# Backward attention scores with 64 streamed columns: a zero-padded dO that slides over eight output columns

## The chip, the core and the metric

The kernel runs on one NeuronCore of a Trainium2 chip. The time is the device time of one launch in microseconds (us). Six runs of the kernel before took 1149.5 to 1152.5 us, with a median of 1151.64 us. Lower is better.

The core has four engines that compute, each with its own in-order queue: TensorE (called PE in the profile, with its weight loads as PEld), VectorE (DVE), ScalarE (ACT) and GpSimd (POOL). SyncE (SP) issues the loads here, and POOL issues the stores. A matmul on PE is two instructions: a weight load of `lhsT`, and the matmul, which streams the columns of `rhs` past the weights and writes as many columns into PSUM.

## The reference

A small decoder with two layers that share their weights, batch 2, one query token, is run forward and then differentiated. Each layer is a grouped-query attention over a cache of 16384 keys, and an MLP. What is returned is the output and the gradients of nine inputs, the two caches among them.

```python
def _A_ref(x, k_cache, v_cache, wq, wo):          # Hq = 32, Hkv = 4, Sk = 16384, Dh = 128
    q = (x @ wq).reshape(B, Sq, Hq, Dh).transpose(0, 2, 1, 3)
    k = jnp.repeat(k_cache, rep, axis=1)           # rep = 8: eight query heads share a key head
    v = jnp.repeat(v_cache, rep, axis=1)
    scores = jnp.einsum("bhqd,bhkd->bhqk", q, k) * (Dh ** -0.5)
    p = _softmax(scores, axis=-1)
    o = jnp.einsum("bhqk,bhkd->bhqd", p, v)
    return o.transpose(0, 2, 1, 3).reshape(B, Sq, Hq * Dh) @ wo

x = x + _A_ref(_layernorm(x), ...)                 # layer 0
x = x + _B_ref(_layernorm(x), ...)                 # layernorm, gelu MLP
x = x + _A_ref(_layernorm(x), ...)                 # layer 1, same caches and weights
x = x + _B_ref(_layernorm(x), ...)
...
_out, _vjp = jax.vjp(_f, A_x, A_k_cache, A_v_cache, A_wq, A_wo, B_w1, B_b1, B_w2, B_b2)
```

The part that matters here is the backward pass through layer 1's attention. With dO the gradient of `o`, each key t of a head needs dP[h, t] = dO[h] . V[t], and from it dS = p * (dP - delta), and dq = sum over t of dS[h, t] K[t].

## The kernel before, in words

The work is cut by group: `g` is one pair of batch and key head, so there are G = 8 groups, and each holds eight query heads. A group's cache of 16384 keys by 128 is read in NCH = 4 chunks of 1 MB ([128 partitions, 32 blocks, 128]), a chunk is worked in NB = 4 slots, and a slot is eight blocks of 128 keys. The whole of layer 1's attention backward is `attn_bwd` (L597 to L713), and it has 8 x 4 x 4 = 128 slots. It runs from 504 us to 660 us of the profiled execution.

What a turn `s` of its loop emits, in the order in which PE's queue gets it:

1. `emit_T` (L420): eight transposes of the V chunk's blocks into one PSUM bank (L424, a matmul of 128 columns each, with the V block as weights and the identity streamed), and a copy of that bank to SBUF as `kT`, on ACT (L158) or DVE (L161), whichever a running charge of costs finds freer.
2. On every third turn one of the 16 transposes of a kept V chunk (`v_turns`, L326).
3. `sch.run_slot`: what was put off to this turn, most of all one `quad` of the dq sums (L456, eight matmuls of 256 columns with K as the streamed operand).
4. `score(s - 2)` (L670): the scores of the slot of two turns ago. Eight weight loads of `kT` blocks, and eight matmuls that stream dO of the group, eight columns, one for each head.
5. Once a chunk is complete, `post` (L638): one matmul that subtracts delta (L640), and one DVE multiplication that makes dS (`dX`, L646).
6. Work on the gradient of the normed input, as dot products on DVE (L343) and some transposes on PE (L326), taken from the queues `wq_q` and `dots`.

The last group, G - 1, has its V chunks held in SBUF (`keepV`, transposed in place), so its 16 slots need no transpose in this stage and are put between those of the third and fourth groups of the list.

The scores of a slot are written as follows; `sc[g, c]` is one PSUM bank seen as [128 keys of a block, 8 heads, 32 blocks], so that the eight results of a block are 32 floats apart:

```python
PE.matmul(sc[g, c][:, :, b * 8 + j], lhsT=kT[:, j, :], rhs=do_bf[:, g, :], start=(b + j == 0), stop=False)
```

K and V chunks, chunks of `wq` and later of the MLP's weights all take turns in NLD = 7 buffers of 1 MB (the pool `ld`). SP issues a load when its buffer's last reader is done: for a V chunk that is the last transpose of L424, for a K chunk the last matmul of L456, for a `wq` chunk the last dot of L343 with its sum (L617). The order of all this is written out by hand; nothing plans it at build time except the choice between ACT and DVE for copies.

Elsewhere the kernel streams more columns than it needs: in the products with weights (`wide_in` and `wide_out`, L175 to L181, used in L285, L367, L385 and L904) the two columns of the two batch rows are repeated 16 times, 32 columns in all.

Of the kernel before, what the change touches and what calls it, by code (L numbers as in the profile page):

```python
# [9 lines left out]
BF16 = mybir.dt.bfloat16  # L10
# [13 lines left out]
def kernel(  # L24
# [24 lines left out]
    nc = tc.nc  # L49
    V = nc.vector  # L50
    S = nc.scalar
    PE = nc.tensor
# [11 lines left out]
    G = B * HKV  # L64
# [14 lines left out]
    vec = ctx.enter_context(tc.tile_pool(name="vec", bufs=1))  # L79
# [12 lines left out]
    def pt(shape, dtype, name):  # L92
        return ps_tp.tile(shape, dtype, name=name, tag="tp")

    def px(shape, dtype, name):
        return ps_x.tile(shape, dtype, name=name, tag="x")
# [59 lines left out]
    def evac_bf16(dst, src, n):  # L156
        if pick() == "A":
            S.copy(out=dst.bitcast(I32), in_=src.bitcast(I32))  # L158
            charge("A", 0.17 + n / 2 / 1200.0)
        else:  # L160
            V.tensor_copy(out=dst, in_=src)  # L161
            charge("D", 0.16 + n / 1920.0)
# [159 lines left out]
    def turn(view, new_tp):  # L322

        tp = new_tp()
        for o in range(8):
            PE.transpose(tp[:, o, :], view[:, o * 128:(o + 1) * 128], ident[:])  # L326
        evac_bf16(view, tp[:].rearrange("p a b -> p (a b)"), 1024)
# [76 lines left out]
    def kept_vT(c):  # L404

        return held_tiles["V%d" % c][:].rearrange("p (t d) -> p t d", d=128)

    def kv_load(w, g, c):
        keep = w + str(c) if g == G - 1 else w if (g, c) == (XG, 0) else None
        t = held_tiles[keep] if keep else ld.tile([128, LDW], BF16, name="kv_" + w, tag="ld")  # L410
        if keep not in held:
            src = Kv if w == "K" else Vv
            nc.sync.dma_start(t[:].rearrange("p (t d) -> p t d", d=128), src[g, :, c * TC:(c + 1) * TC, :])
            if keep:
                held.add(keep)
        return t[:].rearrange("p (t d) -> p t d", d=128)
# [3 lines left out]
    def emit_T(cv, b, third):  # L420
        tp_n["n"] += 1
        tp = (px if third and tp_n["n"] % 3 == 0 else pt)([128, 8, 128], BF16, "tp")
        for j in range(8):
            PE.transpose(tp[:, j, :], cv[:, b * 8 + j, :], ident[:])  # L424
        kT = ktp.tile([128, 8, 128], BF16, name="kT", tag="kT")
        evac_bf16(kT[:].rearrange("p a b -> p (a b)"), tp[:].rearrange("p a b -> p (a b)"), 1024)
        return kT
# [169 lines left out]
    def attn_bwd(l, do_bf, dqT, dn, groups, ahead):  # L597
# [3 lines left out]
        for i, g in enumerate(groups):  # L601
            for c in range(NCH):
                for b in range(NB):
                    slots.append((g, c, b))
                    if 2 <= i < 2 + NCH // 2 and c % 2 == 0:
                        slots.append((G - 1, (i - 2) * 2 + c // 2, b))
        kTs, sc, accs = {}, {}, {}
        made = {"n": 0}
        done_g = []
        dots = deque()  # L610
# [27 lines left out]
        def post(g, c):  # L638
            dp = sc.pop((g, c))
            PE.matmul(dp[:].rearrange("p h t -> p (h t)"), lhsT=hot3[:],  # L640
                      rhs=dlr[:, g, l, :].unsqueeze(2).to_broadcast([128, 8, TC]), start=False, stop=True)
            k = made["n"]
            made["n"] += 1
            ds = dXr[k // 2 % 3][:, :, k % 2]
            ev = e_all[:, g, c * CP:(c + 1) * CP, l, :, :].rearrange("p a h b -> p h a b")
            V.tensor_tensor(out=ds.rearrange("p a h b -> p h a b"),  # L646
                            in0=dp[:].rearrange("p h (a b) -> p h a b", b=2), in1=ev, op=ALU.mult)
            charge("D", 0.5)
            if c == 0:
                def finish(ps, g=g):  # L650
                    V.tensor_scalar(out=dqT[:, g, :], in0=ps, scalar1=QSCALE, scalar2=None, op0=ALU.mult)
                    done_g.append(g % HKV)
                    if g == groups[-1]:
                        wq_n[g % HKV][1]()
                        wq_n[g % HKV][3]()
                    elif done_g.count(g % HKV) == 2:
                        by_dots(g % HKV)
                accs[g] = Acc(g, "K", None, finish, 2 if g == G - 1 else groups.index(g) % 2)
            acc = accs[g]
            if g == groups[-1]:  # L660
                accs[g].pre[c] = kv_load("K", g, c)
                if c == NCH - 1:
                    for k in range(NLD - 2):
                        ahead.load(k)
                        j0, rb = ahead.chunks[k]
                        w2_q.extend(lambda j=j: ahead.row(j) for j in range(j0, j0 + rb))
            coef = lambda u: ds[:, u - c * CP].rearrange("p h t -> p (h t)")
            sch.later(2, lambda: queue_acc(sch, acc, [c], c == NCH - 1, coef))

        def score(s):  # L670
            g, c, b = slots[s]
            if b == 0:
                sc[g, c] = px([128, 8, TC], F32, "dp")
            kT = kTs.pop(s)
            for j in range(8):
                PE.matmul(sc[g, c][:, :, b * 8 + j], lhsT=kT[:, j, :], rhs=do_bf[:, g, :], start=(b + j == 0),
                          stop=False)
            if b == NB - 1:
                post(g, c)

        cv = None
        s = 0
        v_turns = deque(lambda c=c, b=b: turn(held_tiles["V%d" % c][:, b * 1024:(b + 1) * 1024],
                                              lambda: pt([128, 8, 128], BF16, "turn"))
                        for c in range(NCH) for b in range(NB))
        while s < len(slots) + 2 or sch.busy():
            sch.s = s
            if s < len(slots):
                g, c, b = slots[s]
                if g == G - 1:  # L690
                    kTs[s] = kept_vT(c)[:, b * 8:(b + 1) * 8, :]
                else:
                    if b == 0:
                        cv = kv_load("V", g, c)
                    kTs[s] = emit_T(cv, b, True)
                    if s % 3 == 2 and s >= 8 and v_turns:
                        v_turns.popleft()()
                if g == groups[-1] and b == 1 and c == 0:
                    n = wq_n[g % HKV] = wq_steps(l, g % HKV, dqT, dn, lambda: pt([128, 8, 128], BF16, "wtq"),
                                                 lambda: px([128, 512], F32, "dn_ps"))  # L700
                    for k, f in enumerate(n[0]):
                        wq_q.append(lambda f=f, k=k, n=n: (f(), n[2][4 * k]()))
                        wq_q.extend(n[2][4 * k + 1:4 * k + 4])
            sch.run_slot(1 if s < len(slots) else 2)
            if 2 <= s < len(slots) + 2:
                score(s - 2)
            if wq_q and (s % 2 == 1 or len(wq_q) > 6):
                wq_q.popleft()()
            if dots and s % 3 < 2:
                dots.popleft()()  # L710
            s += 1
# [174 lines left out]
    def wq_steps(l, kv, dqT, dn, new_tp, new_ps, get_=None, done_=lambda *job: None):  # L886

        hs = slice(kv * 8, kv * 8 + 8)
        box = {}

        def load(j):
            wt = ld.tile([128, LDW], BF16, name="wqt", tag="ld") if get_ is None else get_("wq", kv, j)
            box[j] = wt[:].rearrange("p (j n) -> p j n", j=4)
            if get_ is None:
                nc.sync.dma_start(box[j], wq_v[:, j:j + 4, kv * D:(kv + 1) * D])

        def turn_row(j):
            turn(box[j - j % 4][:, j % 4, :], new_tp)

        def products(j0=0):  # L900
            ps = new_ps()
            for j in range(j0, DJ):
                for o in range(8):
                    PE.matmul(wide_out(ps, 2 * j), lhsT=box[j - j % 4][:, j % 4, o * 128:(o + 1) * 128],  # L904
                              rhs=wide_in(dq_all[:, kv * 8 + o, 2 * l:2 * l + 2]), start=(o == 0), stop=(o == 7))
            V.tensor_tensor(out=dn[:, j0:DJ], in0=dn[:, j0:DJ],
                            in1=ps[:, 2 * j0:2 * DJ].rearrange("p (j b) -> p j b", b=2), op=ALU.add)
            for j in (0, 4):
                done_("wq", kv, j)

        def dq_in():
            for b in range(2):
                V.tensor_copy(out=dq_all[:, hs, 2 * l + b], in_=dqT[:, b * HKV + kv, :])

        return [lambda j=j: load(j) for j in (0, 4)], dq_in, [lambda j=j: turn_row(j) for j in range(DJ)], products, box
# [353 lines left out]
    kTs, dps, accs, ready = {}, {}, {}, []  # L1269
# [126 lines left out]
    while 2 * m < NS + 12 or late or fill or late_pe or m <= max(v_at) + 2:  # L1396
# [6 lines left out]
        for k in range(2):  # L1403
            s = 2 * m + k
            if s < NS:
                i, b = NCH + s // NB, s % NB
                cv = get("V", *chunks[i])[:].rearrange("p (t d) -> p t d", d=128)
                kT = ktp.tile([128, 8, 128], BF16, name="kT", tag="kT")
# [55 lines left out]
```

## Time and profile before

| What | Value |
|---|---|
| Median of the runs (range) | 1151.64 us (1149.5 to 1152.5) |
| The profiled execution's own time | 1150.81 us |
| Its span (first to last instruction) | 1149.0 us |
| Mean granted PE clock over the span | 0.825 |
| Busy share of the span: PE, PEld, DVE, ACT, POOL | 83%, 64%, 55%, 49%, 6% |
| HBM read and written | 348.14 MB and 98.58 MB, 389 GB/s over the span |
| `attn_bwd`, matmuls of L676 | 896 from `kT` and 128 from `keepV`, 1024 in all, 504.4 to 657.2 us |

How to read it: the 1149.0 us are the span of one execution, which took 1150.81 us as a run, 1.81 us more than the span; the median of the six runs is 0.83 us above that run. A row of the windows view gives the length of a stretch and then the busy time of PE, PEld, DVE, ACT and POOL (with the number of instructions in brackets), the granted PE clock as a share of full speed, the busy share of the DMA engines, and GB/s. In the timeline a row is a start, a length, the engine, line and operation, and how many instructions are merged into it. The ends of matmuls are modelled, and each is longer than the spacing of two of them, so the spacing is read from starts: the start of one row against the start of the next.

### The profile page before, as it was taken

What the parts mean: (1) busy time and instruction counts of PE and PEld (TensorE: products, weight loads), DVE (VectorE), ACT (ScalarE), POOL (GpSimd) and SP (SyncE); (2) the same over time, 40 slices, a digit from 0 to 9 for tenths busy, and PEclk for the clock granted to TensorE, in tenths of its full rate; (3) what the DMA queues carried; (4) which work ended last, traced back from release to release, by engine and by line L of the source; (5) the groups of instructions that cost most, each with busy time, mean ns of one, the idle gap of its engine ahead of it and who ended that gap; (6) DMA issues with size and microseconds to landing.
All of it is one profiled execution on the core that took longest, in us unless ns stands there. A gap on an engine that the chain in (4) does not pass through costs nothing. (4 is left out here: it accounts for less than half of the span.)

```text
span 1149.0 us, 39958 instructions
## 1 busy us (share of the span) xinstructions
PE 958.0 (83%) x17581; PEld 733.0 (64%) x17581; DVE 632.4 (55%) x1335; ACT 566.9 (49%) x1417; POOL 63.7 (6%) x113
## 2 busy tenths in 40 slices
PE   4989795488879875899996889788898999999785
PEld 3867673487767765888775688665555555555452
DVE  1535451133535433454845355668777877786784
ACT  0544351022535430344554455657677867786673
POOL 0000000000000000000000000001111112111111
PEclk9988895597989875899998799888758967796785
DMA  9999999998999989999999999877999999999996
GB/s 374 423 424 425 425 424 412 408 362 366 423 424 416 423 310 424 387 357 406 366 421 420 357 357 359 322 292 295 383 416 416 421 422 420 424 423 419 423 422 253
DMA packets 89130, 449.30 MB, mean 391 GB/s; under 512 B 7026, under 2 KB 7026, under 8 KB 49788
## 3 DMA queue, kind: packets, MB, share of 16 engines
q1 hardware_dynamic: 72204, 348.17, 75.0%
q0 software_dynamic: 16752, 98.59, 20.7%
q8 instruction: 137, 2.24, 0.7%
q14 instruction: 37, 0.30, 0.1%
HBM read 348.14 MB, written 98.58 MB: 389 GB/s over the span
## 5 line engine op out<-in xcount | busy, mean ns | idle before, releaser
L158 ACT COPY kT<-tp 128x512 int32<-128x512 int32 x209 | 122.6, 586 | 253.6 <-PE tp L424 242.5
L161 DVE COPY kT<-tp 128x1024 bf16<-128x1024 bf16 x159 | 108.6, 690 | 113.0 <-PE tp L424 98.6
L424 PE MATMUL tp<-ident,kv_K 128*128 128x128 bf16 x1728 | 146.0, 234 | 4.2 <-DMA kv_K<-in_A_k_cache_dram 4.2
L424 PEld LDWEIGHTS <-kv_K 128*128 128x128 bf16 x1728 | 110.9, 105 | 5.0 <-DMA kv_K<-in_A_k_cache_dram 4.8
L169 DVE CAST big<-xm 128x512 bf16<-128x512 f32 x142 | 92.5, 685 | 28.9 <-PE xm L1242 13.3
L166 ACT CAST big<-xm 128x512 bf16<-128x512 f32 x155 | 84.5, 592 | 25.7 <-PE xm L1144 14.7
L577 PEld LDWEIGHTS <-kT 128*128 128x128 bf16 x2048 | 76.6, 98 | 28.6 <-issue 23.6
L577 PE MATMUL sc<-qT_bf,kT 128*128 128x8 bf16 x2048 | 92.1, 171 | 1.3 <-issue 1.3
L274 PE MATMUL wtp<-ident,wt 128*128 128x128 bf16 x928 | 76.4, 230 | 4.0 <-issue 2.5
L424 PE MATMUL tp<-ident,kv_V 128*128 128x128 bf16 x864 | 70.8, 230 | 8.6 <-DMA kv_V<-in_A_v_cache_dram 7.4
L541 ACT ACTIVATE e_all<-sc,negm 128x64 bf16<-128x64 f32 x256 | 76.9, 343 | 1.1 <-DVE negm L536 1.0
L310 PEld LDWEIGHTS <-wt 128*128 128x128 bf16 x1696 | 48.9, 103 | 44.2 <-issue 14.7
L169 DVE CAST keepK<-xm 128x512 bf16<-128x512 f32 x95 | 61.6, 684 | 16.5 <-PE xm L1242 10.7
L161 DVE COPY wT<-wtp 128x1024 bf16<-128x1024 bf16 (+1 forms) x64 | 40.5, 637 | 47.8 <-PE wtp L274 44.7
L456 PE MATMUL acc_all<-kv_V,e_all 128*16 128x256 bf16 x864 | 46.0, 293 | 24.8 <-DVE acc_all L439 12.3
L158 ACT COPY wT<-wtp 128x512 int32<-128x512 int32 (+1 forms) x60 | 34.5, 575 | 64.5 <-PE wtp L274 55.7
L166 ACT CAST keepK<-xm 128x512 bf16<-128x512 f32 x102 | 54.8, 592 | 21.8 <-PE xm L1242 21.1
L166 ACT CAST keepV<-xm 128x512 bf16<-128x512 f32 (+1 forms) x98 | 53.1, 592 | 22.1 <-PE xm L1242 19.9
L424 PEld LDWEIGHTS <-kv_V 128*128 128x128 bf16 x864 | 56.0, 102 | 10.5 <-DMA kv_V<-in_A_v_cache_dram 8.2
L274 PEld LDWEIGHTS <-wt 128*128 128x128 bf16 x928 | 58.6, 103 | 4.7 <-issue 3.4
L541 ACT ACTIVATION_READ_ACCUMULATOR e_all<-sc,negm 128x1 f32 x256 | 60.0, 235 | 0.0
L169 DVE CAST keepV<-xm 128x512 bf16<-128x512 f32 (+1 forms) x74 | 47.9, 684 | 16.7 <-PE xm L1242 12.8
(352 smaller groups left out, 1778.4 us busy)
## 6 DMA issues: line engine op xcount, KB each, us to landing
kv_K<-in_A_k_cache_dram SPq DMA_DIRECT2D x81, 1024.0 KB, 12.3
kv_V<-in_A_v_cache_dram SPq DMA_DIRECT2D x81, 1024.0 KB, 12.0
out_dram<-big POOLq DMA_DIRECT2D x36, 1024.0 KB, 16.1
wt<-in_A_wo_dram SPq DMA_DIRECT2D x32, 1024.0 KB, 9.3
wt<-in_B_w_dram SPq DMA_DIRECT2D x32, 896.0 KB, 14.2
out_dram<-keepK POOLq DMA_DIRECT2D x22, 1024.0 KB, 16.2
out_dram<-keepV POOLq DMA_DIRECT2D x18, 1024.0 KB, 15.8
wt<-in_A_wq_dram SPq DMA_DIRECT2D x16, 1024.0 KB, 8.6
```

Of the source, the lines that this page charges most:

```text
L158: S.copy(out=dst.bitcast(I32), in_=src.bitcast(I32))
L161: V.tensor_copy(out=dst, in_=src)
L166: S.copy(out=dst, in_=src)
L169: V.tensor_copy(out=dst, in_=src)
L274: PE.transpose(tp[:, o, :], wv[:, j, (o0 + o) * 128:(o0 + o + 1) * 128], ident[:])
L310: PE.matmul(fps[:, jo, :].rearrange("p (a b) -> p a b", b=2), lhsT=wv[:, j, jo * 128:(jo + 1) * 128], rhs=xT_bf[:, j0 + j, :].unsqueeze(1) ...
L424: PE.transpose(tp[:, j, :], cv[:, b * 8 + j, :], ident[:])
L456: PE.matmul(self.acc[cg:cg + 16, :], lhsT=coef(u), rhs=self.cv[:, t:t + 2, :].rearrange("p t d -> p (t d)"), start=False, stop=True, tile_ ...
L541: S.activation(out=e_all[:, g, f * half:(f + 1) * half, l, h, :], in_=sc[g][f][:, h, :].rearrange("p (a b) -> p a b", b=2), func=ACT.Exp, ...
L577: PE.matmul(sc[g][f][:, :, t % TH], lhsT=kT[:, j, :], rhs=q_bf[:, g, :], start=True, stop=True)
```

## The change

Three zeroed tiles `wide` of [128, 8 heads, 15] take the place of dO as the streamed operand. Two of them serve the seven groups that load V, in turn, and one serves the group G - 1. At the first slot of a group, DVE copies the group's dO into the middle column, number 7, of each head's 15. For block j the matmul streams columns 7 - j to 14 - j of each head: eight columns, of which the one at place j is dO and the others are zero. The output is then all eight columns of the slot for all eight heads, 64 columns, and each of the slot's eight matmuls adds onto the same 64 places of PSUM. Weight loads, the number of matmuls, the order of PE's queue and all loads and stores stay as they were.

```diff
-        kTs, sc, accs = {}, {}, {}
+        kTs, sc, accs, wide = {}, {}, {}, {}
+        for i, g in enumerate([G - 1] + groups):
+            wide[g] = vec.tile([128, 8, 15], BF16, name="wz%d" % i) if i < 3 else wide[groups[i - 3]]
+            if i < 3:
+                nc.gpsimd.memset(wide[g][:], 0.0)
...
             for j in range(8):
-                PE.matmul(sc[g, c][:, :, b * 8 + j], lhsT=kT[:, j, :], rhs=do_bf[:, g, :], start=(b + j == 0),
-                          stop=False)
+                PE.matmul(sc[g, c][:, :, b * 8:b * 8 + 8], lhsT=kT[:, j, :], rhs=wide[g][:, :, 7 - j:15 - j],
+                          start=(b + j == 0), stop=False)
...
+        wide_made = set()
...
                 if g == G - 1:
                     kTs[s] = kept_vT(c)[:, b * 8:(b + 1) * 8, :]
-                else:
+                if g not in wide_made:
+                    wide_made.add(g)
+                    V.tensor_copy(out=wide[g][:, :, 7], in_=do_bf[:, g, :])
+                if g != G - 1:
                     if b == 0:
                         cv = kv_load("V", g, c)
                     kTs[s] = emit_T(cv, b, True)
```

Lines after the first hunk move down by four, later ones by eight: the scores of L676 stand in L680 of the changed kernel.

## The prediction

> **What bounds the kernel now.** I first split the stage that holds the changed line by the windows view (columns: length, busy PE, PEld, DVE, ACT, POOL, PE clock, DMA share, GB/s), then asked for PE's waits in each part.
>
> ```profile
> 504.00:587.00 83.00, 79.64 (x1734) 65.71 (x1732) 47.34 (x106) 39.34 (x70) 0.00 (x0) 0.98 0.96 381
> 587.00:652.00 65.00, 49.45 (x915) 41.03 (x912) 35.50 (x78) 29.86 (x54) 0.00 (x0) 0.84 0.99 404
> 652.00:660.00 8.00, 7.43 (x137) 5.28 (x137) 0.42 (x1) 3.76 (x7) 0.00 (x0) 0.79 0.94 334
> ```
>
> PE's longest waits, with total, count and longest one; the first two of 504 to 587 us, the last two of 587 to 652:
>
> ```profile
> PE dp L676 <- DVE kT L161: 1.1, 1, 1.1
> PE acc_all L456 <- DVE acc_all L439: 0.7, 1, 0.7
> ...
> PE tp L424 <- DMA kv_V<-in_A_v_cache_dram: 7.4, 4, 3.7
> PE acc_all L456 <- DMA kv_K<-in_A_k_cache_dram: 2.9, 3, 1.3
> ```
>
> So the stage has three parts. To 587 PE never waits for a load: PE is the bound. From 587 to 652 it waits 12.3 us for loads (2.0 us on `wq` beside these two), with DMA at 0.99: the loads are the bound. From 652 on PE is busy 7.43 of 8 us again and ends the stage; its clock is 0.79.
>
> Where does PE's lateness in the first part reach the loads? Where DMA runs dry:
>
> ```profile
> 552.00:560.00 8.00, 7.92 (x177) 6.48 (x173) 6.89 (x15) 5.08 (x9) 0.00 (x0) 1.00 0.78 275
> 562.50:565.00 2.50, 2.50 (x65) 2.01 (x61) 2.43 (x6) 1.15 (x4) 0.00 (x0) 1.00 0.90 341
> 653.80:657.20 3.40, 3.40 (x57) 2.33 (x54) 0.00 (x0) 1.27 (x3) 0.00 (x0) 0.50 0.96 377
> ```
>
> The last dry stretch before the part bound by loads ends at 565 us. What PE is late by then moves all loads behind it; later lateness, up to the 640s, is taken up by PE's waits.
>
> **The price of 64 columns.** The timeline gives starts; the next row's start closes a set of eight.
>
> ```profile
> 551.26 0.36 PE L676 MATMUL dp<-doT_bf,kT 128*128 128x8 bf16 x8
> 551.47 0.34 PE L676 MATMUL dp<-doT_bf,keepV 128*128 128x8 bf16 x8
> 551.67 0.61 PE L424 MATMUL tp<-ident,kv_V 128*128 128x128 bf16 x8
> 552.12 0.61 PE L326 MATMUL turn<-ident,keepV 128*128 128x128 bf16 x8
> ...
> 487.10 0.36 PE L285 MATMUL do_ps_b<-gA_all,wT 128*128 128x32 bf16 x8
> 487.30 0.61 PE L274 MATMUL wtp<-ident,wt 128*128 128x128 bf16 x8
> ...
> 612.96 1.01 PE L424 MATMUL tp<-ident,kv_V 128*128 128x128 bf16 x8
> 613.77 0.41 PE L676 MATMUL dp<-doT_bf,kT 128*128 128x8 bf16 x8
> 614.03 0.37 PE L640 MATMUL dp<-dlr,hot 128*128 128x256 bf16 x1
> ```
>
> Eight score matmuls take 0.205 us (0.21 and 0.20), as do eight of 32 columns (0.20): below some width a matmul costs 25 ns whatever it streams. Eight of 128 columns take 0.45 us, 56 ns each. No row has 64. Half of 56 is 28, and 29 with a small fixed part: 0.23 us for eight, +0.03. The straight line between the rows of 32 and 128 gives 35 ns, +0.08. I take 29, for the 128-column row looks like pure streaming. At half clock (the last three rows) eight transposes take 0.81 us and eight scores 0.26; eight of 64 would take about 0.41, +0.15.
>
> A rule speaks against the change. The Trainium skill's "Advanced Engine Details and Errata", section "Memory Cachelines", says that the array's reads want at least two hits on a 16-byte line of SBUF, and that non-contiguous PSUM access slows matmuls, pairs being best. The new operand is read in runs of eight bf16 with 15 from run to run, mostly across a line's edge: two lines for each run instead of one. Were each line paid, 64 columns would cost twice, 56 ns, +0.25 us for eight. Against it stands the row: scores written one float at a time, 32 apart, already run at 25 ns, no slower than the contiguous L285, and the new writes are runs of eight. Nearly every line gets two hits or more. By the row the first part costs 1.9 us, by the rule 15; I keep the row, and the rule as a rival.
>
> **The change part by part.**
>
> 1. *Streaming, first part.* To 565 us the stage starts 496 score matmuls, 62 sets, all at clock 1.00: 62 x 0.03 = 1.9 us. PE has no cover there. Bounds: 0 (loads queued ahead absorb it) to 62 x 0.08 = 5.0 us. The 23 sets from 565 to 587 add 0.7 us of PE, covered by the load waits after 587.
>
> 2. *Streaming, second part.* About 39 sets, 1 to 4 us of PE, beside 12.3 us of waits for loads: nothing. If that cover went, it would be those 4 us.
>
> 3. *Streaming, tail.* From 640 us on DMA is dry at times (0.86 in 640.2 to 643.6) because buffers wait for PE. There lie four sets at half clock, 4 x 0.15 = 0.6 us.
>
> 4. *Eight DVE copies* of dO, 128x8 into a strided place. Nearest row: the cast L913, 128x8, 174 ns. Seven stand in DVE's queue two turns before PE needs them: nothing on PE, 1.2 us on DVE (47.34 of 83 us busy; it is full only around 555 to 575). The first one is different:
>
> ```profile
> 504.39 0.36 PE L676 MATMUL dp<-doT_bf,kT 128*128 128x8 bf16 x8
> 504.60 0.61 PE L424 MATMUL tp<-ident,kv_V 128*128 128x128 bf16 x8
> 505.42 0.27 DVE L942 MEMSET w2b_f<- 128x256 f32 x1
> 505.60 1.26 DVE L161 COPY kT<-tp 128x1024 bf16<-128x1024 bf16 x2
> 506.33 0.33 PE L676 MATMUL dp<-doT_bf,kT 128*128 128x8 bf16 x7 [1.12 <-DVE kT L161]
> ```
>
> DVE is in the delta chain (L870 to L882) until 505.1 and then clears two tiles. In the built order the first copy comes behind these and ahead of the `kT` copies. Until now the first scores waited for ACT's `kT` alone, at 504.39; now they wait for DVE, about 505.70 + 0.17, so 505.9. Queued behind them on PE are eight transposes (0.45 us) and the second scores, at 506.33 today because PE waits 1.12 us for DVE anyway: 505.9 + 0.23 + 0.45 = 506.6. So 1.5 us of new wait costs +0.3 us; late next are the transposes' buffers and with them loads, in a stretch where DMA is not full. Bounds 0.1 (the DVE copy alone) to 0.7.
>
> 5. *Three POOL memsets.* Emitted behind POOL's last work at 437.7 us, before the store at 700.53: idle engine, nothing; without that cover under a microsecond each (POOL's smallest rows take 0.5 to 0.7).
>
> No DMA, SP or ACT instruction is added or moved, and PE's queue keeps its order.
>
> **Sum.** 0.3 + 1.9 + 0.6 = 2.8 us. The profiled execution took 1150.81 us (span 1149.0 and 1.81 around it): 1153.6. The median is 0.83 us above it: **1154.4 us**, +0.24%. Everything after 660 us starts from this stage's gradient, so I pass the delay on whole.
>
> **The clock.** The low steps of the granted clock last multiples of 3.4 us and follow stretches where PE streams little. The skill's "TensorE: Matmul & The Clock Gate", Part 1, states such a window and that activity lifts the clock; columns streamed in zeros are activity too. By the row nothing changes; by the rule some of these steps go. Counted from the trace for the window before 653.8: 16 transposes, a 256-column matmul and a quad (four at a time) stream about 2800 columns of the 7800 that fit at 56 ns for 128, 36%; one wide set there adds 448, to 42%. The same count over the whole trace has windows that keep full clock from 35% up and windows that lose it up to 44%: undecided. What one saved step is worth: in the tail two sets of transposes (0.71 and 0.94 us against 0.45 each) and two quads (0.54 against 0.32 each), 1.2 us.
>
> **Rivals.**
>
> - *The tail stays warm.* Part 3 falls to 0.1 and 1.2 us come back: 0.3 + 1.9 + 0.1 - 1.2 = +1.1, **1152.7**, within 0.2%. For it: the 42%. Against: one set can miss the window.
> - *Faster: the clock.* The steps at 571.9, 640.2 and 653.8 all go, 3 x 1.2 = 3.6 us, and loads queued ahead absorb part 1's streaming (a K or V load lands 12 us after its issue, so there is a queue): 0.3 - 3.6 = -3.3, **1148.3**. It decides where the lateness that reaches the loads stays below about 1 us. Against: DMA did run dry at 552 to 560, and faster PE in the middle gains nothing.
> - *Dear columns.* 35 ns gives 5.0 + 0.3 + 1 = 6.3, **1158**; the line rule at 56 ns gives 15 + 0.3 + 2, **1169**. For it: the rule, and no row of 64. Against: flat cost to 32 columns.
>
> That the change does not do what it says is excluded: the built list shows 1024 matmuls of 8x8 columns in the old places.
>
> **How the numbers follow.** Under 0.2% (2.3 us, 1149.3 to 1153.9) a measurement of this kernel tells nothing apart. Forecast 0.40 (own range 1153.2 to 1156.5, 0.30 of it above 1153.9); tail warm 0.27; faster 0.18; dear columns 0.15. So slower 0.30 + 0.15 = 0.45, same 0.10 + 0.27 = 0.37, faster 0.18. For eight in ten the range takes half of the faster case and the cheaper half of the dear one: 1148.5 to 1160.
>
> **What would show it.** Starts of eight wide scores 0.23 us apart at full clock (0.28 or more speaks for dear columns); the first scores near 505.9; DMA drier around 552 to 560 by nearly 2 us, PE's waits for loads after 587 shorter by 1 to 4 us; the stage's end near 662.5. Fewer half-clock steps between 568 and 658 speak for the clock rivals. The forecast is wrong if the loads' queue hides the first part, or if the clock settles the tail.

## The result and the profile after

The changed kernel is slower. Its median is 1157.86 us (15 runs, 1153.55 to 1160.73) against 1151.79 us of the kernel before in the same series. The ratio over all runs is 1.0045, with a 95% interval of 1.0033 to 1.0058: +5.2 us on the time before, from 3.8 to 6.7 (the two medians alone lie 6.1 us apart). The forecast was 1154.4, +2.8. The sign and the range (1148.5 to 1160) held, but the loss is nearly twice the forecast's, and above the forecast's own range of 1153.2 to 1156.5.

The profiled execution took 1157.91 us, its span is 1156.1 us (before: 1149.0) and its mean granted clock 0.826 (0.825). I measured the changed stage from the start of the second of its two delta matmuls (L864, now L872; 502.94 us before, 503.94 after) to the first of the 64 products with `wq` that follow the last scores (L904, now L912; 661.14 and 666.82). It took 158.2 us before and 162.9 us after, +4.7. The other 2.4 us of these two executions lie outside: 1.0 before the stage, where only the three memsets are new (0.47 us in all, on an idle POOL), and 1.4 behind it, where nothing is.

The windows view of the profile after, with the columns of before, cut at the same three parts of the stage:

```profile
505.00:588.00 83.00, 80.73 (x1671) 67.93 (x1669) 46.86 (x107) 37.32 (x66) 0.00 (x0) 1.00 0.93 361
588.00:656.40 68.40, 53.17 (x979) 45.33 (x977) 36.74 (x85) 31.84 (x58) 0.00 (x0) 0.89 1.00 405
656.40:664.00 7.60, 7.60 (x113) 5.82 (x113) 0.42 (x1) 2.68 (x5) 0.00 (x0) 0.64 0.84 278
```

In the same 83 us PE gets through 1671 matmuls instead of 1734, is busy longer (80.73 for 79.64), and DMA moves 361 GB/s instead of 381. The parts keep their bounds: PE first, then the loads (DMA 1.00), then PE alone at a low clock.

PE's waits after, the first three in 505 to 588 us (the whole list there), the last two the longest waits on K and V in 588 to 656.4:

```profile
PE dp L680 <- DVE wz L699: 1.3, 1, 1.3
PE acc_all L456 <- DVE acc_all L439: 0.7, 1, 0.7
PE o_ps L471 <- DVE dX L650: 0.2, 1, 0.2
...
PE tp L424 <- DMA kv_V<-in_A_v_cache_dram: 8.1, 4, 3.7
PE acc_all L456 <- DMA kv_K<-in_A_k_cache_dram: 2.1, 3, 0.9
```

The first line is the new wait for the dO copy. It stands where the wait of 1.1 us for DVE's `kT` stood. No other wait came in in this part. Two waits of the list before (504 to 587 us) shrank; the second of them lies ahead of 565 us:

```profile
PE o_ps L471 <- DVE dX L646: 0.6, 1, 0.6
PE tp L424 <- DVE kT L161: 0.6, 1, 0.6
```

The timeline of PE after: two wide sets at full clock, with the row that closes them, and one at half clock.

```profile
553.07 0.45 PE L680 MATMUL dp<-wz,kT 128*128 128x64 bf16 x8
553.35 0.43 PE L680 MATMUL dp<-wz,keepV 128*128 128x64 bf16 x8
553.62 0.61 PE L339 MATMUL dotr<-ident,dq_all 128*128 128x128 bf16 x8
...
658.72 0.61 PE L680 MATMUL dp<-wz,kT 128*128 128x64 bf16 x8
659.14 1.04 PE L424 MATMUL tp<-ident,kv_V 128*128 128x128 bf16 x8
```

Eight scores take 0.28 and 0.27 us, 34 ns a matmul, where the forecast had 29. At half clock they take 0.42, as forecast (0.41). In the median of the stage's sets at full clock it is 0.277 us against 0.213, +0.064: 62 sets are 4.0 us instead of 1.9.

How late PE is can be read directly. The 63rd set of scores is the first behind 565 us; its row before, and after:

```profile
565.15 0.36 PE L676 MATMUL dp<-doT_bf,kT 128*128 128x8 bf16 x8
```

```profile
569.91 0.44 PE L680 MATMUL dp<-wz,kT 128*128 128x64 bf16 x8
```

Counted from the delta matmul it starts at 62.21 us before and at 65.97 after: PE is 3.76 us late at the end of the part in which the forecast gave it no cover. This is the main reading. The working comes out: 62 x 0.064 = 4.0, and 0.2 of the first wait, less 0.4 that the old wait for DVE's `kT` gave back (0.57 us before, 0.13 after).

The start of the stage in the timeline after:

```profile
506.60 0.17 DVE L699 COPY wz<-doT_bf 128x8 bf16<-128x8 bf16 x1
506.62 0.68 DVE L161 COPY kT<-tp 128x1024 bf16<-128x1024 bf16 x1
506.83 0.44 PE L680 MATMUL dp<-wz,kT 128*128 128x64 bf16 x8 [1.27 <-DVE wz L699]
...
507.55 0.44 PE L680 MATMUL dp<-wz,kT 128*128 128x64 bf16 x8
```

The first scores start 2.89 us after the delta matmul, before it was 1.46: 1.43 us late, as the forecast had it (1.5). The second scores start 3.61 us after it, before it was 3.40: 0.2 us are left of the wait.

Where DMA ran dry, in the windows view before:

```profile
552.00:565.00 13.00, 12.92 (x297) 10.10 (x293) 11.78 (x24) 7.33 (x14) 0.00 (x0) 1.00 0.85 316
```

And after, the same 13 us of the stage (it starts 1.0 us later), and the low clock in the tail:

```profile
553.00:566.00 13.00, 12.99 (x280) 10.57 (x273) 10.13 (x22) 6.22 (x11) 0.00 (x0) 1.00 0.74 273
655.10:661.90 6.80, 5.53 (x64) 4.32 (x64) 0.35 (x3) 2.16 (x4) 0.00 (x0) 0.50 0.70 237
```

DMA's share in these 13 us fell from 0.85 to 0.74, which is 1.4 us of all queues. SP issues the loads later, for it waits for PE's reads: of the 25 us from 546 on it waited 11.3 us for L456 and 9.3 for L424. The last loads of this stretch, before and after:

```profile
563.98 1.61 SPq L413 DMA_DIRECT2D kv_K<-in_A_k_cache_dram  x2
```

```profile
568.30 2.05 SPq L413 DMA_DIRECT2D kv_K<-in_A_k_cache_dram  x2
```

From the delta matmul that is 61.04 and 64.36 us: the loads are 3.3 us late as well. The low step of the clock at 571.9 is gone, but the one in the tail is 6.8 us long instead of 3.4.

### The profile page after: what moved, and what is told of

It is laid out like the page before. It is cut to its first block, busy times and chain, and to the rows that moved or that the text cites. A ratio compares the mean times of both kernels' runs of the same rounds, so it can differ in the third digit from the quotient of the medians.

```text
span 1156.1 us, 39970 instructions
## 1 busy us (share of the span) xinstructions
PE 966.2 (84%) x17581; PEld 744.3 (64%) x17581; DVE 633.7 (55%) x1343; ACT 567.1 (49%) x1417; POOL 64.2 (6%) x116
## 3 DMA queue, kind: packets, MB, share of 16 engines
q0 software_dynamic: 16752, 98.59, 20.5%
## 5 line engine op out<-in xcount | busy, mean ns | idle before, releaser
L424 PE MATMUL tp<-ident,kv_K 128*128 128x128 bf16 x1728 | 146.5, 235 | 3.3 <-DMA kv_K<-in_A_k_cache_dram 3.2
L424 PEld LDWEIGHTS <-kv_K 128*128 128x128 bf16 x1728 | 111.3, 105 | 4.0 <-DMA kv_K<-in_A_k_cache_dram 3.8
L424 PE MATMUL tp<-ident,kv_V 128*128 128x128 bf16 x864 | 68.9, 225 | 9.2 <-DMA kv_V<-in_A_v_cache_dram 8.1
L456 PE MATMUL acc_all<-kv_V,e_all 128*16 128x256 bf16 x864 | 46.2, 294 | 28.4 <-DMA kv_V<-in_A_v_cache_dram 16.9
L166 ACT CAST keepV<-xm 128x512 bf16<-128x512 f32 (+1 forms) x98 | 53.1, 593 | 20.5 <-PE xm L1250 18.6
L424 PEld LDWEIGHTS <-kv_V 128*128 128x128 bf16 x864 | 55.3, 101 | 10.8 <-DMA kv_V<-in_A_v_cache_dram 9.5
```

The source lines that it names most:

```text
L166: S.copy(out=dst, in_=src)
L456: PE.matmul(self.acc[cg:cg + 16, :], lhsT=coef(u), rhs=self.cv[:, t:t + 2, :].rearrange("p t d -> p (t d)"), start=False, stop=True, tile_ ...
```

## The experiments

The expectations set theories against each other: that the price of the streamed columns is the loss; that it is the wait and the copies; that it is where the new tiles push everything behind them in SBUF. All ratios are to the kernel before on the same chip. "A set" is eight score matmuls of a slot at full clock, "the stage" as measured above, and "late" is how much later the 63rd set starts after the delta matmul than in the kernel before. The diffs are cut to what matters; `...` marks what is left out.

### Eight columns again, the rest of the change kept

```diff
-                PE.matmul(sc[g, c][:, :, b * 8:b * 8 + 8], lhsT=kT[:, j, :], rhs=wide[g][:, :, 7 - j:15 - j],
+                PE.matmul(sc[g, c][:, :, b * 8 + j], lhsT=kT[:, j, :], rhs=wide[g][:, :, 7],
```

> The changed kernel with eight streamed columns again, read from the middle column of the padded tile; the eight DVE copies, the three memsets and the new wait of the first scores stay. Theory S (streaming of 64 columns on PE, 34 ns a matmul against 25.6, is the loss): eight scores take 0.205 us, the time is that of the kernel before plus 0.3 us, about 1152. Rival W (the copies and waits on DVE are the loss): it stays near the changed kernel, about 1157.

Measured: 1154.0 us, ratio 1.0031 (1.0017 to 1.0046). A set takes 0.22 us and the wait of 1.3 us for `wz` is there. The result lies between the theories. In its profile PE is only 0.4 us late (the single elements 15 apart are a little slower than the 0.21 of before, and 0.15 us of the wait is left); the interval of the loss begins at 2.0 us. The stage took 160.2 us, +1.9, and the work outside it 3.3 us more than in the profile before, so that most of this execution's loss lies where nothing was changed. Where it comes from stays open. The run shows that narrow columns take away nearly all of PE's lateness; how much of the time they take back it does not show.

### Half as many columns

```diff
-            wide[g] = vec.tile([128, 8, 15], BF16, name="wz%d" % i) if i < 3 else wide[groups[i - 3]]
+            wide[g] = vec.tile([128, 8, 7], BF16, name="wz%d" % i) if i < 3 else wide[groups[i - 3]]
...
-                PE.matmul(sc[g, c][:, :, b * 8:b * 8 + 8], lhsT=kT[:, j, :], rhs=wide[g][:, :, 7 - j:15 - j],
+                t0, k = b * 8 + j - j % 4, 3 - j % 4
+                PE.matmul(sc[g, c][:, :, t0:t0 + 4], lhsT=kT[:, j, :], rhs=wide[g][:, :, k:k + 4],
...
```

> The padded tile is seven wide, and a matmul streams 32 columns (four output columns of each head). Theory S: below the floor of 25 ns width is free, eight scores take 0.205 us, about 1152. Rival R (the padded layout costs, not the width: runs that cross lines): 28 ns or more a matmul, 1154 to 1156. Rival C (the granted clock, lifted by padded columns, moves the time): fewer half-clock steps than before, and a time below 1151.

Measured: 1163.26 us, ratio 1.0101 (1.0078 to 1.0123). No theory of the stage expected this. A set takes 0.21 us, so 32 columns cost no more than eight. But the stage starts at 508.9 us instead of 502.9: six microseconds were lost before the first changed score ran. What differs there is the size of the padded tiles, and with it the address of everything allocated behind them. That led to the two runs with an unused tile further down.

### Which layout costs: operand contiguous, PSUM in single floats

```diff
-            wide[g] = vec.tile([128, 8, 15], BF16, name="wz%d" % i) if i < 3 else wide[groups[i - 3]]
+            wide[g] = vec.tile([128, 15, 8], BF16, name="wz%d" % i) if i < 3 else wide[groups[i - 3]]
...
-                PE.matmul(sc[g, c][:, :, b * 8:b * 8 + 8], lhsT=kT[:, j, :], rhs=wide[g][:, :, 7 - j:15 - j],
-                          start=(b + j == 0), stop=False)
+                PE.matmul(sc[g, c][:, :, b * 8:b * 8 + 8].rearrange("p h t -> p t h"), lhsT=kT[:, j, :],
+                          rhs=wide[g][:, 7 - j:15 - j, :], start=(b + j == 0), stop=False)
...
```

> 64 columns, but the padded tile is laid out with the heads innermost, so each matmul reads 64 neighbouring elements; its PSUM writes are then single floats 32 apart. Theory S with the width alone as cause: 34 ns a matmul as in the changed kernel, about 1158. Rival R (the operand's runs across lines cost): 29 ns, eight scores in 0.23 us, about 1154.5. Rival P (PSUM places apart cost): more than 34 ns, over 1160.

Measured: 1169.39 us, ratio 1.0154 (1.0129 to 1.0180), stage 175.3 us. PE's timeline:

```profile
560.62 0.62 PE L680 MATMUL dp<-wz,kT 128*128 128x64 bf16 x8
561.05 0.64 PE L680 MATMUL dp<-wz,keepV 128*128 128x64 bf16 x8
```

The starts are 0.43 us apart, 54 ns a matmul (53.8 in the mean over the stage at full clock): the same 64 columns, each written to a float 32 floats from the last, cost nearly twice 29. It is also a dose run. With +0.22 a set the kernel lost 17.7 us instead of 5.2. PE is 13.8 us late, which is 62 x 0.22 and 0.2 of wait; the rest comes later, for PE's first wait of over 0.4 us for a load comes only 122 us into the stage (before: 90). The time follows the price of the set.

### Both contiguous

```diff
-            wide[g] = vec.tile([128, 8, 15], BF16, name="wz%d" % i) if i < 3 else wide[groups[i - 3]]
+            wide[g] = vec.tile([128, 15, 8], BF16, name="wz%d" % i) if i < 3 else wide[groups[i - 3]]
...
-                sc[g, c] = px([128, 8, TC], F32, "dp")
+                sc[g, c] = px([128, TC, 8], F32, "dp")
...
-                PE.matmul(sc[g, c][:, :, b * 8:b * 8 + 8], lhsT=kT[:, j, :], rhs=wide[g][:, :, 7 - j:15 - j],
-                          start=(b + j == 0), stop=False)
+                PE.matmul(sc[g, c][:, b * 8:b * 8 + 8, :], lhsT=kT[:, j, :],
+                          rhs=wide[g][:, 7 - j:15 - j, :], start=(b + j == 0), stop=False)
...
```

The delta matmul (L644) and the multiplication (L650) read the bank in its new order; the multiplication takes 422 ns as before.

> 64 columns, operand and PSUM writes both contiguous (the scores' bank is laid out block by block with the heads innermost; the DVE product reads it with a stride). Width alone: 34 ns, about 1158. Rivals R or P: 29 ns, about 1154.5; together with the run that has only the operand contiguous this tells which of the two.

Measured: 1154.6 us, ratio 1.0020 (1.0007 to 1.0034), stage 159.3 us. A set takes 0.24 us, with matmuls 29.0 ns apart in the median: the forecast's price is right for contiguous columns. The same copies, the same wait, the same 64 columns, and PE is 1.6 us late instead of 3.8; the ratio fell by about half.

### Is it the address? An unused tile

```diff
+    spare = vec.tile([128, 384], BF16, name="spare")
+    nc.gpsimd.memset(spare[:], 0.0)
     x1 = attn_layer_fwd(0, xT0)
```

In the kernel before, 768 bytes a partition of it put the load buffers 256 bytes past a multiple of 512, where the change put them; 384 bytes put them 384 past one. In the changed kernel and in the contiguous one, 256 bytes put them back on a multiple of 512; the runs of the next three sections carry these 256 bytes too.

> The kernel before with one unused tile of 768 bytes a partition, which moves the load buffers, caches and work tiles up by as much as the three padded tiles do in the changed kernel (start of the buffers 256 past a multiple of 512). Theory S (streaming is the whole loss): no change, 1151.5. Rival A (where the load buffers start matters): slower, by up to the 2.7 us that the run with eight columns was over the kernel before.

> The kernel before with one unused tile of 384 bytes a partition, which moves the load buffers as the 32-column version does (384 past a multiple of 512). Theory S: no change, 1151.5. Rival A: about 1161 to 1163, for the 32-column version took 1163 although its matmuls were at 25 ns, and its 8 KB packets took 312 to 321 ns against 309 before.

> The changed kernel with 256 bytes more, so that the load buffers start at a multiple of 512 again, as before. Theory S: no change, 1157.9. Rival A: down by what the address costs, to 1155 to 1156; what is left over the kernel before is streaming and the new wait.

> 64 columns with operand and PSUM contiguous, and the load buffers at a multiple of 512. By my sum with 29 ns a matmul: 2.8 us over the kernel before with the tail at half clock, 1154; 1.1 us over with the tail warm, 1152.7. Rival A says it is below the same version without the extra 256 bytes (1154.6).

Measured: 768 bytes in the kernel before, 1151.7 us, 1.0002 (0.9988 to 1.0016). The changed kernel put back, 1155.71 us, 1.0044 (1.0028 to 1.0059), the same ratio as without. So no part of this change's loss is seen to come from the address. Put back, its profile loses in the stage nearly what the first one did (162.2 us, before 158.2; PE is again 3.8 us late), while the work outside the stage takes 991.2 us against 990.8.

384 bytes, in a kernel with no other change: 1166.3 us, 1.0130 (1.0103 to 1.0157). The windows view of one stretch ahead of the stage, before and with 384 bytes:

```profile
100.00:400.00 300.00, 240.87 (x5087) 204.88 (x5086) 120.15 (x282) 106.03 (x446) 2.07 (x3) 0.81 1.00 409
```

```profile
100.00:400.00 300.00, 238.06 (x5010) 201.77 (x5007) 117.88 (x275) 103.88 (x442) 2.07 (x3) 0.81 0.99 402
```

The DMA is as busy and moves 1.7% less, where the loads are the bound. The run with half as many columns has its buffers at the same place and moved 403 GB/s there; the address accounts for what it lost ahead of the stage.

The contiguous kernel put back: 1154.86 us, 1.0029 (1.0016 to 1.0043), +3.3 us. PE's timeline:

```profile
551.14 0.41 PE L680 MATMUL dp<-wz,kT 128*128 128x64 bf16 x8
551.38 0.40 PE L680 MATMUL dp<-wz,keepV 128*128 128x64 bf16 x8
```

The starts are 0.24 us apart. The prediction's sum, 2.8 us, was made with about this price (0.23), and the kernel with this price lost 2.3 and 3.3 us in its two forms. The number agrees; its parts are less sure. PE is 1.6 us late in both profiles, and the stages (159.3 and 159.8 us) are hardly longer than in kernels that lose nothing (158.9 to 159.6, below).

### PSUM contiguous, operand in single elements

```diff
-                PE.matmul(sc[g, c][:, :, b * 8:b * 8 + 8], lhsT=kT[:, j, :], rhs=wide[g][:, :, 7 - j:15 - j],
+                PE.matmul(sc[g, c][:, b * 8:b * 8 + 8, :], lhsT=kT[:, j, :],
+                          rhs=wide[g][:, :, 7 - j:15 - j].rearrange("p h t -> p t h"),
...
```

The bank is laid out as in the contiguous kernel.

> 64 columns with contiguous PSUM writes, but the operand read one element at a time, 15 apart (columns outer, heads inner, over the changed kernel's padded tile); load buffers at a multiple of 512. Theory P (places apart in PSUM make a matmul dear, the operand's layout does not): 29 ns, eight scores in 0.23 us, time as with both contiguous, 1154.9. Rival R (the operand's layout does): over 34 ns, for every element lies on another line, and 1158 or more.

Measured: 1226.27 us, ratio 1.0661 (1.0632 to 1.0690). PE's timeline:

```profile
563.70 1.09 PE L680 MATMUL dp<-wz,kT 128*128 128x64 bf16 x8
564.61 0.65 PE L680 MATMUL dp<-wz,keepV 128*128 128x64 bf16 x4
```

0.91 us a set, 114 ns a matmul. PE is 46 us late and bounds nearly the whole stage: of its waits for loads (14.9 us before) 1.4 us are left, behind 200 us of the stage. The idea that only the PSUM side can cost fell: elements of the operand 15 apart cost four times what contiguous ones do. Where the granted clock was 0.50 a matmul took 117 ns, nearly the same.

### The copies alone

The change's tiles, memsets and copies are in; the scores still stream eight columns of dO and wait for no copy.

```diff
+                if g not in wide_made:
+                    wide_made.add(g)
+                    V.tensor_copy(out=wide[g][:, :, 7], in_=do_bf[:, g, :])
```

> Memsets and the eight copies of the changed kernel, but the scores stream dO itself, eight columns, and wait for no copy; load buffers at a multiple of 512. Theory S: as the kernel before within 0.5 us, 1151.7. Rival W (the copies' own time on DVE is a part of the loss): as the run with eight columns from the padded tile, 1153 to 1154.5.

Measured: 1152.4 us, ratio 1.0010 (0.9993 to 1.0026), stage 158.9 us. Copies and memsets cost nothing that can be measured; the interval's ends are -0.8 and +3.0 us. PE is not late at all (0.0 us). The interval overlaps that of the run with eight columns from the padded tile.

### Wide scores in the last three groups only

```diff
+                if g in groups[4:]:
+                    PE.matmul(sc[g, c][:, :, b * 8:b * 8 + 8], lhsT=kT[:, j, :], rhs=wide[g][:, :, 7 - j:15 - j],
+                              start=(b + j == 0), stop=False)
+                else:
+                    PE.matmul(sc[g, c][:, :, b * 8 + j], lhsT=kT[:, j, :], rhs=do_bf[:, g, :], start=(b + j == 0),
+                              stop=False)
...
```

The first wide set is the 81st; only these groups' dO is copied.

> The changed kernel's scores and copies for the last three groups alone (48 of 128 slots, from about 575 us on); the first four and the last group stream eight columns without a copy; load buffers at a multiple of 512. Theory S with its place (lateness counts where loads run dry, before 565 us, and in the tail): 0.5 to 1.5 us over the kernel before, 1152 to 1153. If it counts everywhere alike: 48/128 of the 5 us, 1153.5; if the clock in the tail is lifted and that is worth 1.2 us: at or under 1151.

Measured: 1152.38 us, ratio 1.0007 (0.9989 to 1.0024), stage 159.2 us. This agrees with the view that PE's lateness counts only ahead of the part bound by loads. The time does not prove it: were the loss spread evenly over all sets, 48 of 128 would bring 0.17%, which the interval holds as well. The profile says more: at the 94th set PE is 1.1 us behind the run with the copies alone, and at the 98th only 0.1, for in between that run waits 1.2 us for a load of K and this one does not. What PE was late went into the wait.

### A version without the dear parts

32 columns, both sides contiguous, and one copy of all groups' dO made before the delta chain, so that PE meets no new wait.

```diff
-        delta(l, delta_mm(l, dof))
+        bank = delta_mm(l, dof)
+        V.tensor_copy(out=wide_all[:, :, 3, :], in_=dof[:])
+        delta(l, bank)
...
-                PE.matmul(sc[g, c][:, :, b * 8 + j], lhsT=kT[:, j, :], rhs=do_bf[:, g, :], start=(b + j == 0),
-                          stop=False)
+                t0, k = b * 8 + j - j % 4, 3 - j % 4
+                PE.matmul(sc[g, c][:, t0:t0 + 4, :], lhsT=kT[:, j, :], rhs=wide_all[:, g, k:k + 4, :],
+                          start=(b + j == 0), stop=False)
```

> Meant as the best of both: 32 columns, operand and PSUM contiguous, all groups' padded dO made by one copy straight from the scaled gradient while PE works on delta, so no new wait; load buffers at a multiple of 512. By the floor of 25 ns streaming costs nothing: the stage is as long as before, 158 to 159 us, and the time 1151 to 1152; if the padded columns lift the clock where it counts, 1150. If it is at 1154, something other than streaming, waits and addresses costs.

Measured: 1150.21 us, ratio 0.9996 (0.9981 to 1.0011), a set 0.21 us, stage 159.6 us. It takes the loss away and gains nothing that can be measured: streaming more columns is of no use here even when PE pays nothing for it. In its profile PE is 1.2 us late all the same, most of it from one stop of 1.0 us in which it waited for nothing that the profile shows; lateness of this size does not show in the time. No version tried beats the kernel before.

## Why the prediction was right in sign and short in size

**What bounds the stage: held.** The three parts kept their bounds, and PE's lateness at the end of the first part goes with the price of a set:

| Scores | A set, us | 63rd set late by, us | Ratio |
|---|---|---|---|
| Eight columns: 768 bytes unused, copies alone, late groups | 0.21 | 0.0, 0.0, 0.0 | 1.0002, 1.0010, 1.0007 |
| Eight columns from the padded tile | 0.22 | 0.4 | 1.0031 |
| 64, both contiguous, two forms | 0.24 | 1.6, 1.6 | 1.0020, 1.0029 |
| 64, the change, two forms | 0.28 | 3.8, 3.8 | 1.0045, 1.0044 |
| 64, PSUM in single floats | 0.43 | 13.8 | 1.0154 |
| 64, operand in single elements | 0.91 | 46.1 | 1.0661 |

The table leaves out the two kernels with their buffers 384 bytes past a multiple of 512 (0.45 and 1.25 us late) and the version without the dear parts (1.2), all at 0.21 us a set.

DMA ran drier where I put it, by 1.4 us there and by 2.5 over the first part (its share fell from 0.96 to 0.93 of 83 us), where I said nearly 2. PE's waits for loads in the stage shrank from 14.9 to 13.9 us, the low end of the 1 to 4 I named; the unused 768 bytes moved them to 15.7, so this sign is a weak one.

**The price of 64 columns: the step that failed.** "I take 29, for the 128-column row looks like pure streaming", and then "I keep the row, and the rule as a rival". A set cost +0.064 us, not +0.03. PE was to be 0.3 + 1.9 = 2.2 us late by 565 us and was 3.76. With the forecast's 0.6 for the tail that is 4.4, where the stage grew by 4.7 and, put back, by 4.0, and the ratio gives 5.2 (3.8 to 6.7). The first half of the step was right: contiguous columns measured 29.0 ns. The second was a wrong reading of a row. I took the old scores, single floats 32 apart at 25 ns, as evidence that PSUM's layout costs nothing. The run with single floats shows 54 ns for 64 of them, 0.84 ns a column. By this, an estimate, eight such columns are 7 ns, far below the 25 ns that a matmul takes anyway. A row that is held by a floor cannot show what lies under it.

The rule that I set against the row, from the Trainium skill's "Advanced Engine Details and Errata", section "Memory Cachelines" (two hits on a line of SBUF, pairs in PSUM), was right in direction on both sides: single floats in PSUM nearly doubled the price, single elements of the operand made it fourfold. Paid in full, as in the rival of 56 ns, it was far too much for the changed kernel, whose runs are of eight on both sides. Which of the two sides makes 34 out of 29 there was not tried by itself: no run changes one from runs of eight to contiguous and leaves the other as it is.

**The dear rival** came nearest in number: it put 35 ns at 1158. Its reason, the straight line between 32 and 128 columns, is refuted by the 29.0 of the contiguous kernel; that its 35 ns came so near the measured 34 is luck.

**The first wait: held.** 1.43 us late, 0.2 left one slot later (forecast 1.5 and 0.3), because PE waited for DVE there anyway. That the next such wait would shrink too, by 0.4 us, was in no term of the sum.

**Streaming in the second part: nothing, as far as seen.** The run with wide scores in the last three groups only is no different from before; its interval reaches +2.8 us. In its profile a wait for a load took PE's lateness up.

**The tail: right price, no sum to be read.** A set at half clock took 0.42 to 0.44, as forecast. In this execution two of the four sets fell into a low step, and that step lasted 6.8 us. From the end of the last `wq` wait to the end of the stage it took 10.5 us instead of 9.0; but it took 9.5 in the changed kernel put back, and 9.9 and 10.1 with the unused 768 bytes and with the copies alone, which have no wide column. The forecast's +0.6 can't be told from this.

**Copies and memsets: held**, at nothing that can be measured. That the delay passes whole to the end of the program is consistent with the padded version, where the time outside the stage differs by 0.4 us.

**The clock rivals: refuted as to time.** Time at half clock in the stage fell from 27.3 to 20.5 us in the two profiles (17.1 in the changed kernel put back, 13.7 in both contiguous ones; 23.9 with the unused 768 bytes and with the copies alone). The direction is that of the rule I weighed, the Trainium skill's "TensorE: Matmul & The Clock Gate", Part 1, that activity lifts the clock. But the steps that went, at 571.9 and 599.2, went with the unused 768 bytes as well and lay where loads are the bound, and the one in the tail grew. That faster PE in the middle gains nothing, the argument against the faster rival, is what happened.

**What stays open.** Eight columns out of the padded tile lost 2.0 to 5.3 us where PE is 0.4 us late, and the contiguous kernels 2.3 and 3.3 us in the middle of their intervals where PE is 1.6 late. PE's lateness at the end of the first part is shown to come from the price of the columns; passed on whole it makes 3.8 of the 5.2 us lost. What the other 1.4 are, if they are more than scatter, is not known.

## What to carry to other kernels

A narrow matmul runs at a floor (25 ns here, up to 32 columns), and at the floor its width does not show and its layout hardly (27 ns for eight single elements 15 apart); before widening it, price the wider form from a row that is above the floor and has the same strides on both sides. If a wide operand is wanted, make both the streamed operand and the PSUM result contiguous: 64 columns cost 29 ns so, 34 in runs of eight on both sides, 54 with single floats in PSUM and 114 with single elements of the operand. And columns that are streamed as zeros bought nothing here: they cost where PE was the bound, and where it was not, less time at half clock gained nothing. To see what a dearer instruction costs, follow the start of one and the same set through the profiles: here that agreed to 0.02 us between two forms of one kernel, where the time of a run moved by several microseconds.

## What the runs showed of the hardware that was not expected

- *An address can cost 1.3% of the whole kernel.* An unused tile of 384 bytes a partition, placed ahead of the load buffers, made the kernel 15 us slower (1.0130), while one of 768 bytes did nothing (1.0002). In 100 to 400 us an 8 KB packet of the loads took 312 ns in the median, and eight in ten took 309 to 319, where before it was 309. The caches and `kT` move with the load buffers, so which of them matters is not separated; the longer packets point to the buffers. A change that adds a tile should be compared with the same program with an unused tile of that size.
- *The streamed operand has a price of its own.* 64 bf16 elements 30 bytes apart took 114 ns at full clock and 117 at half clock, so that the granted clock hardly mattered; 64 contiguous ones took 29 and 55.
- *The same program moves by a microsecond.* The stage took 158.2 us in the profile of before, 159.2 with the harmless 768 bytes and 158.9 with the copies alone. A single profile's stage says nothing below that.
